# One decode layer on one core: K and V in three rotating 8 MiB tiles of four heads instead of four 4 MiB tiles of two

## The chip, the cores and the metric

One core of a Trainium2 chip runs the whole layer as one program. The metric is the device time of one execution in microseconds (us); the median of three runs counts. A profiled execution comes with it: its own time, and a trace whose times run from the start of the span, that is from the core's first to its last recorded instruction. TensorE is called PE (its weight loads PEld), VectorE DVE, ScalarE ACT, GpSimd POOL, and SyncE, which issues nearly all DMAs, SP.

## The reference

A decode step for batch 2 and one new token: attention over a cache of 8192 keys, with 32 heads of 128, then a gated feed-forward. All inputs are bf16. Cut to what matters:

```python
# x [2,1,512]; k_cache, v_cache [2,32,8192,128]; wq [512,4096]; wo [4096,512]
q = layernorm(x) @ wq                                   # 32 heads of 128
p = softmax(einsum("bhqd,bhkd->bhqk", q, k_cache) * 128 ** -0.5)
h = x + einsum("bhqk,bhkd->bhqd", p, v_cache) @ wo
hn = layernorm(h)                                       # W_gate, W_up [512,1376], W_down [1376,512]
gate = hn @ W_gate
out = h + (gate * (gate > 0) * (hn @ W_up)) @ W_down
```

K and V are 134 MB each and are read once. They are 268 of the 281 MB that the core loads.

## The kernel before

**Steps and tiles.** A step is a pair of heads of one batch entry: 32 steps, `i` = 0 to 31, the last called `L`. The K of a pair is 4 MiB and lies as 128 partitions of 32 KiB (`ROW`): heads side by side in the partitions (64 each), 128 keys (`NT`) of 128 numbers in each partition. `kbuf` and `vbuf` hold two such tiles each, so K of step `i + 2` goes where K of step `i` lay.

**Scores.** Most of the keys of a partition are scored on DVE, in place in the K tile: `products` (L335) multiplies by the query, `scores` (L350) adds halves four times, and a reduction (L354) makes the scores. The rest, 16 of 128 keys (24, 32 and 8 in some steps at the ends), go over PE in `scores_pe`: transposed in chunks of eight (L309), copied by ACT (L311), multiplied by a query laid out with zeros (L300), copied as rows (L316), transposed back (L319) and copied into the column of scores (L325).

**Softmax and values.** A reduction (L358), a matmul (`largest`, L365) and a second reduction (L377) give the largest score; `exponentials` (L380) writes the weights on ACT. `values` multiplies weights and V with 32 matmuls of 512 columns a step, in two parts (L396); ACT copies the result (L402). For each group of four steps `diagonals` (L411) picks the heads out of it, `sums` (L266) adds up the exponentials on PE, `shares` (L270) takes the reciprocal on DVE, and `normalise` (L274) writes the head's columns `ocol`, on DVE too.

**The order of the work is written out by hand**, and every engine takes its instructions in program order. In the loop, step `i` does: `sums(i - 2)`, `scores_pe(i)`, `products(i)`, `shares` and `normalise` of `i - 2` where a group ended there, `values(i - 1, 0)`, `scores(i)`, `largest`, `exponentials`, the load of K for `i + 2`, `values(i - 1, 1)`, `diagonals(i - 1)`, the load of V for `i + 1`. The values are thus one step, and the normalising two steps, behind the scores. All these loads go through SP's queue in order (L133); each first waits until the work that reads or writes the old data of its place is done.

**The weights.** W_q is loaded first, into `wbig`, and W_o after it into the same place while the first K tiles land. W_o is cut into sets (`SETS`): one of 128 KiB lies on 16 partitions only, in four rows of four (L240), the others on 128. `spread` and `attend_set` bring the heads into the matching layout and multiply. After the loop come the last step, with V in four pieces, and the loads of W_gate, W_up and W_down (L522, L526), then the rest of the attention, the second norm and the feed-forward. `values_cols` (L423) does the values of the last two steps with V as the stationary operand.

Of the kernel before, what the change touches and what calls it, by code (L numbers as in the profile page):

```python
# [23 lines left out]
def kernel(  # L24
# [13 lines left out]
    nc = tc.nc  # L38
# [6 lines left out]
    HALF = P // 2  # L45


    NT = 2 * Sk // P
    ROW = NT * Dh
    NG = Hq // 2  # L50
    NPE = NT // 4
    NPE_MID = NT // 8
    NPE_LAST = NT // 16
    TPC = 8
    VG = 4
# [5 lines left out]

    FSETS = [(0, 6), (6 * P, 1), (7 * P, 1), (8 * P, 1), (9 * P, 1), (F - P, 1)]
# [3 lines left out]

    SETS = [(0, 16, P, 0), (16, 1, 16, 16), (17, 1, P, 24), (18, 2, P, 25), (20, 4, P, 27), (24, 4, P, 32)]
    WO_T = 36  # L70
    HM = Hq - 4

    assert Sq == 1 and Hkv == Hq and Dh == P and D == KC * P and Hq == 32 and NPE % TPC == NPE_MID % TPC == NPE_LAST % TPC == 0
    assert F == 11 * P - AGAIN

    big = ctx.enter_context(tc.tile_pool(name="big", bufs=1))
    consts = ctx.enter_context(tc.tile_pool(name="consts", bufs=1))
    small = ctx.enter_context(tc.tile_pool(name="small", bufs=2))
# [3 lines left out]
    big.tile([P, 192], bf16, name="pad")  # L82
    kbuf = big.tile([P, 2, ROW], bf16)
    vbuf = big.tile([P, 2, ROW], bf16)
    wbig = big.tile([P, 40 * D], bf16)
    wd_sb = big.tile([P, FC, D], bf16)
    qrep = consts.tile([P, B, NG, Dh], bf16)

    wq_sb = wbig[:, 0:KC * Hq * Dh].rearrange("p (c n) -> p c n", c=KC)

    wgu = kbuf[:, 0, 0:2 * KC * F].rearrange("p (k c f) -> p k c f", k=2, c=KC)


    pgz = consts.tile([P, 2, NT // VG, 2, VG], bf16)

    pv = consts.tile([P, 2, VG * Dh], f32)
    pick = consts.tile([P, VG, 4, 2], f32)
    zc = consts.tile([P, B, NG, 2], f32)
    ident = consts.tile([P, P], bf16)
    nscale = consts.tile([P, P], f32)  # L100
# [4 lines left out]
    ocol = consts.tile([P, Hq, B], bf16)  # L105
    hm = consts.tile([P, FC, B], bf16)

    SROWS = [n * Dh // w for _, n, w, _ in SETS]
    sizes = [r for r in sorted(set(SROWS)) if r > 1]
    quot = {r: consts.tile([P, Dh // r], bf16, name=f"quot{r}") for r in sizes}  # L110
    rest = {r: consts.tile([P, r], bf16, name=f"rest{r}") for r in sizes}
    orow = [consts.tile([P, r, B], bf16, name=f"orow{k}") for k, r in enumerate(SROWS)]
    placed = consts.tile([P, B, 16], bf16)
    sel = consts.tile([B, B, HALF], bf16)

    QZ = 2 * NPE // 4
    qz = consts.tile([P, B, NG, 2 * QZ], bf16)
    ident_f = consts.tile([QZ, QZ], f32)
# [3 lines left out]

    steps = [(b, g) for b in range(B) for g in range(NG)]
    N = len(steps)

    def wo_set(k):
        return wbig[:, SETS[k][3] * D:]

    def load_kv(cache, buf, i, pieces=1, which=None):
        b, g = steps[i]  # L130
        w = ROW // pieces
        for k in range(pieces) if which is None else which:
            nc.sync.dma_start(  # L133
                out=buf[:, i % 2, k * w:(k + 1) * w],
                in_=_dram(cache, (b * Hkv + 2 * g) * Sk * Dh + k * w, [[ROW, P], [1, w]]),
            )
# [19 lines left out]
    with tc.manual_schedule():  # L156

        xr = wd_sb[0:B, FC - 2, :]
        nc.scalar.dma_start(out=xr, in_=_dram(A_x, 0, [[D, B], [1, D]]))
        nc.sync.dma_start(out=wbig[:, 0:KC * Hq * Dh], in_=_dram(A_wq, 0, [[KC * Hq * Dh, P], [1, KC * Hq * Dh]]))  # L160
        load_kv(A_k_cache, kbuf, 0)
        load_kv(A_k_cache, kbuf, 1)
        load_kv(A_v_cache, vbuf, 0)
# [18 lines left out]
            base=0, pattern=[[-1, B], [0, HALF]], channel_multiplier=1,  # L182
        )
        nc.gpsimd.memset(qz, 0.0)
        nc.gpsimd.memset(pgz, 0.0)
# [4 lines left out]
            base=0, pattern=[[-1, VG], [-32, 4], [-VG, 2]], channel_multiplier=1,  # L190
# [15 lines left out]
        for r in sizes:  # L206
            nc.vector.tensor_reduce(out=rest[r], in_=_free(ident, 0, [[1, r], [r, P // r]]), axis=AXIS.X, op=ALU.max)
            nc.vector.tensor_reduce(out=quot[r], in_=_free(ident, 0, [[r, P // r], [1, r]]), axis=AXIS.X, op=ALU.max)
# [4 lines left out]

        qrow = vbuf[0:B, 1, 0:Hq * Dh]
        for g0 in range(0, NG, 4):
            for n0 in range(2 * g0 * Dh, 2 * (g0 + 4) * Dh, 4 * Dh):
# [6 lines left out]
            for b in range(B):  # L223
                r_ps = ps2.tile([P, 4, Dh], f32, tag="tp")
                for j in range(2):
                    nc.tensor.matmul(  # L226
                        out=r_ps[j * HALF:(j + 1) * HALF], lhsT=sel[:, b, :],
                        rhs=_free(qrow, (2 * g0 + j) * Dh, [[2 * Dh, 4], [1, Dh]]), start=True, stop=True,
                    )
                nc.scalar.activation(out=qrep[:, b, g0:g0 + 4, :], in_=r_ps, func=ACT.Copy)  # L230
# [3 lines left out]
        nc.vector.tensor_copy(qz[:, :, :, QZ - 2:QZ], qT_ps.rearrange("p (g j) b -> p b g j", j=2))  # L234


        for k, ((h0, n, w, _), r) in enumerate(zip(SETS, SROWS)):
            nc.sync.dma_start(
                out=wo_set(k)[0:w, 0:r * D],
                in_=_dram(A_wo, h0 * Dh * D, ([[r * D, P]] if w == P else [[r * D, 4], [4 * r * D, 4]]) + [[1, r * D]]),  # L240
            )
        nc.sync.dma_start(
            out=wbig[:, WO_T * D:(WO_T + Hq - HM) * D].rearrange("p (h n) -> p h n", n=D),
            in_=_dram(A_wo, HM * Dh * D, [[D, P], [Dh * D, Hq - HM], [1, D]]),
        )

        groups = {}
        for b in range(B):
            for g0 in range(0, NG, 4):
                if b == B - 1 and g0 + 4 == NG:  # L250
                    groups[b * NG + NG - 3] = (b, g0, 2)
                    groups[b * NG + NG - 2] = (b, NG - 2, 1)
                    groups[b * NG + NG - 1] = (b, NG - 1, 1)
                else:
                    groups[b * NG + g0 + 3] = (b, g0, 4)
        o_ps = {}
        rzs = {}

        z_ps = {}

        def sums(i):

            if i in groups:
                b, g0, n = groups[i]
                z_ps[i] = ps.tile([P, 2 * n], f32, tag="mx", name="z_ps")
                nc.tensor.matmul(out=z_ps[i], lhsT=ones, rhs=zc[:, b, g0:g0 + n, :], start=True, stop=True)  # L266

        def shares(i):
            rzs[i] = small.tile([P, 2 * groups[i][2]], f32, tag="rz", name="rz")
            nc.vector.reciprocal(out=rzs[i], in_=z_ps[i])  # L270

        def normalise(i):
            b, g0, n = groups[i]
            nc.vector.tensor_tensor(  # L274
                out=ocol[:, 2 * g0:2 * (g0 + n), b], in0=o_ps[i][:, 0:2 * n], in1=rzs[i], op=ALU.mult,
            )

        scols = {}
        L = N - 1

        def share(i):

            npe = NPE_LAST if i == L else NPE if i >= L - 2 else NPE_MID if i else NPE - TPC
            return NT - npe, npe

        def scores_pe(i):


            b, g = steps[i]
            kt = kbuf[:, i % 2, :]  # L290
# [357 lines left out]
```

## Time and profile before

| what | value |
|---|---|
| median of 3 runs | 662.05 us (661.82 to 662.43) |
| profiled execution: its own time, its span | 661.76 us, 660.0 us |
| PE / DVE / ACT / POOL busy | 432.5 / 551.9 / 154.7 / 4.9 us |
| HBM read | 281.09 MB, 426 GB/s over the span |
| K and V loads | 32 of K and 29 of V of 4 MiB, 4 of V of 2 MiB, 4 of V of 1 MiB |
| mean granted TensorE clock | 0.818 of full speed |

Busy times are sums over the whole span, and stages with different limits lie behind them. A PE that is counted busy may be running at half its clock. The 1.76 us between the time and the span lie outside what the trace records.

### The profile page before, as it was taken

The numbers are of one execution on the slowest core, as the hardware profiler recorded it, in microseconds if no ns is written. First come the engines' busy times: TensorE is split into PE (matmuls) and PEld (weight loads), VectorE is DVE, ScalarE is ACT, GpSimd is POOL, SyncE is SP. The second block draws the span as 40 slices with busy tenths as digits, with TensorE's granted clock in tenths as the row PEclk, the third lists the DMA queues.
The fourth block names the chain that finished last, engine by engine and source line by source line (L and its number), as shares of the span: only waits on it lengthen the run. The fifth ranks groups of instructions, "written<-read, shape, count | busy, mean of one in ns | idle before, by whom it ended". The sixth has DMA issues, their size and how long they took to land.

```text
span 660.0 us, 6125 instructions
## 1 busy us (share of the span) xinstructions
PE 432.5 (66%) x2567; PEld 190.8 (29%) x2567; DVE 551.9 (84%) x327; ACT 154.7 (23%) x340; POOL 4.9 (1%) x21
## 2 busy tenths in 40 slices
PE   2725677676666557667656765676676765688676
PEld 1312222322223223222223222232222422234246
DVE  2599998888889888889988888988888998887991
ACT  1421222222122222022222212222221222222410
POOL 2000000000000000000000000000000000000000
PEclk9967987888778898877789877778987778988975
DMA  9999999999999999999999999999999999999996
GB/s 381 434 411 447 427 432 440 420 439 434 429 437 428 437 426 435 439 426 435 436 424 440 427 433 438 427 436 435 425 440 429 430 439 425 439 432 424 430 421 273
DMA packets 13331, 281.48 MB, mean 426 GB/s; under 512 B 1382, under 2 KB 2664, under 8 KB 4200
## 3 DMA queue, kind: packets, MB, share of 16 engines
q1 hardware_dynamic: 13300, 281.09, 99.1%
q8 instruction: 20, 0.33, 0.2%
q14 instruction: 7, 0.06, 0.0%
q10 hardware_dynamic: 4, 0.00, 0.0%
HBM read 281.09 MB, written 0.00 MB: 426 GB/s over the span
## 4 chain that ended last, share of the span: by engine, by line
DMA 52%; DVE 42%; PE 4%; SPq 1%; issue 1%; ACT 0%; DVEq 0%; ACTq 0%
DMA kbuf<-in_A_k_cache_dram 47%; DVE kbuf L350 20%; DVE kbuf L335 19%; DVE scol L354 3%; DMA wd_sb<-in_B_W_down_dram 3%; DMA wbig<-in_A_wq_dram 2%; PE q_ps L219 1%; PE pv_ps L396 1%; SPq L522 1%; DVE vbuf L222 0%; PE r_ps L226 0%; PE mx_ps L365 0%; PE d_ps L606 0%; ACT kT L311 0%; PE row_ps L300 0%
## 5 line engine op out<-in xcount | busy, mean ns | idle before, releaser
L396 PE MATMUL pv_ps<-vbuf,pgz 128*8 128x512 bf16 x960 | 283.5, 462 | 78.0 <-DMA vbuf<-in_A_v_cache_dram 78.0
L335 DVE TENSOR_TENSOR kbuf<-kbuf,qrep 128x14336 bf16<-128x14336 bf16 (+3 forms) x32 | 241.8, 7557 | 40.1 <-DMA kbuf<-in_A_k_cache_dram 40.1
L350 DVE TENSOR_TENSOR kbuf<-kbuf 128x1792 bf16<-128x1792 bf16 (+9 forms) x128 | 242.2, 1892 | 4.1
L396 PEld LDWEIGHTS <-pgz 128*8 128x8 bf16 x960 | 93.3, 100 | 244.1 <-issue 174.5
L380 ACT ACTIVATE pgz<-scol,nm 64x128 bf16<-64x128 f32 x64 | 25.5, 399 | 334.7 <-DVE nm L377 333.9
L311 ACT ACTIVATE kT<-t_ps 128x1024 bf16<-128x1024 bf16 x68 | 66.2, 1021 | 15.1 <-PE t_ps L309 14.6
L300 PE MATMUL row_ps<-kT,qz 128*8 128x512 bf16 (+3 forms) x136 | 42.7, 398 | 33.9 <-ACT kT L311 33.7
L365 PE MATMUL mx_ps<-nscale,pm 128*128 128x128 f32 x64 | 16.5, 343 | 65.4 <-DVE pm L358 63.2
L309 PE MATMUL t_ps<-ident,kbuf 128*128 128x128 bf16 x544 | 37.5, 222 | 0.0
L309 PEld LDWEIGHTS <-kbuf 128*128 128x128 bf16 x544 | 32.1, 100 | 11.8 <-issue 11.7
L354 DVE TENSOR_REDUCE scol<-kbuf 128x112 f32<-128x896 bf16 (+3 forms) x32 | 34.5, 1078 | 1.1
L402 ACT ACTIVATE pv<-pv_ps 8x512 f32<-8x512 f32 x30 | 17.7, 589 | 74.2 <-PE pv_ps L396 74.2
L365 PEld LDWEIGHTS mx_ps<-nscale,pm 128*128 128x128 f32 x64 | 10.5, 206 | 79.9 <-issue 49.0
L377 DVE TENSOR_REDUCE nm<-mx_ps 128x2 f32<-128x128 f32 x32 | 9.3, 291 | 23.8 <-PE mx_ps L365 23.8
L319 PE MATMUL sc_ps<-ident_f,rows 8*128 8x8 f32 (+3 forms) x128 | 14.2, 216 | 21.7 <-ACT rows L316 21.7
L300 PEld LDWEIGHTS <-qz 128*8 128x8 bf16 (+3 forms) x136 | 11.2, 84 | 51.2 <-issue 43.5
L316 ACT ACTIVATE rows<-row_ps 8x512 f32<-8x512 f32 (+3 forms) x32 | 18.8, 587 | 23.4 <-PE row_ps L300 23.4
L319 PEld LDWEIGHTS sc_ps<-ident_f,rows 8*128 8x128 f32 (+3 forms) x128 | 11.3, 149 | 39.5 <-ACT rows L316 39.5
L325 ACT ACTIVATE scol<-sc_ps 64x16 f32<-64x16 f32 (+3 forms) x64 | 12.4, 194 | 17.8 <-PE sc_ps L319 17.0
L222 DVE CAST vbuf<-q_ps 2x512 bf16<-2x512 f32 x8 | 5.4, 678 | 13.2 <-PE q_ps L219 13.2
L219 PE MATMUL q_ps<-wbig,xn 128*2 128x512 bf16 x32 | 9.2, 440 | 8.6 <-DMA wbig<-in_A_wq_dram 8.6
L358 DVE TENSOR_REDUCE pm<-scol 128x1 f32<-128x128 f32 x32 | 9.1, 285 | 3.7 <-DVE scol L354 0.5
(96 smaller groups left out, 112.4 us busy)
## 6 DMA issues: line engine op xcount, KB each, us to landing
kbuf<-in_A_k_cache_dram SPq DMA_DIRECT2D x32, 4096.0 KB, 22.1
vbuf<-in_A_v_cache_dram SPq DMA_DIRECT2D x29, 4096.0 KB, 27.3
vbuf<-in_A_v_cache_dram SPq DMA_DIRECT2D x4, 2048.0 KB, 26.1
wbig<-in_A_wq_dram SPq DMA_DIRECT2D x1, 4096.0 KB, 12.4
vbuf<-in_A_v_cache_dram SPq DMA_DIRECT2D x4, 1024.0 KB, 20.7
wbig<-in_A_wo_dram SPq DMA_DIRECT2D x1, 2048.0 KB, 22.1
wbig<-in_A_wo_dram SPq DMA_DIRECT2D x3, 512.0 KB, 22.1
kbuf<-in_B_W_gate_dram SPq DMA_DIRECT2D x1, 1376.0 KB
```

Of the source, the lines that this page charges most:

```text
L300: nc.tensor.matmul(out=row_ps, lhsT=qz[:, b, g, z0:z0 + 2 * U], rhs=kTs[c0][:, k * P:(k + 4) * P], start=(u == 0), stop=(u == U - 1),)
L309: nc.tensor.transpose(t_ps[:, k, :], kt[:, t * Dh:(t + 1) * Dh], ident)
L311: nc.scalar.activation(out=kTs[c0], in_=t_ps.rearrange("p t s -> p (t s)"), func=ACT.Copy)
L316: nc.scalar.activation(out=rows, in_=row_ps, func=ACT.Copy)
L319: nc.tensor.transpose(sc_ps[:, t].rearrange("p u j -> p (u j)"), rows[:, t * P:(t + 1) * P], ident_f[0:2 * U, 0:2 * U],)
L335: nc.vector.tensor_tensor(out=kv, in0=kv, in1=_free(qrep, (b * NG + g) * Dh, [[0, nv], [1, Dh]]), op=ALU.mult,)
L350: nc.vector.tensor_tensor(out=lo, in0=lo, in1=_free(kt, half, [[Dh, nv], [1, half]]), op=ALU.add,)
L354: nc.vector.tensor_reduce(out=scol[:, 0:nv], in_=_free(kt, 0, [[Dh, nv], [1, 8]]), axis=AXIS.X, op=ALU.add,)
L365: nc.tensor.matmul(out=mx_ps.rearrange("p a b -> p (a b)"), lhsT=_free(pms[i], 0, [[0, P]]), rhs=nscale, start=True, stop=True,)
L380: nc.scalar.activation(out=pgz[r, s, :, j, :], in_=scol[r, :].rearrange("p (u t) -> p u t", t=VG), func=ACT.Exp, scale=SCALE, bias=nm[r, j ...
L396: nc.tensor.matmul(out=pv_ps[i][r, :], lhsT=pgz[:, s, u].rearrange("p j t -> p (j t)"), rhs=vbuf[:, s, u * VG * Dh:(u + 1) * VG * Dh], sta ...
L402: nc.scalar.activation(out=pv[r, (g // 4) % 2], in_=pv_ps[i][r, :], func=ACT.Copy)
```

## The change

A step becomes four heads: a K or V tile is 8 MiB, 64 KiB in each partition (256 keys; a head has 32 partitions). Three tiles `bufs[0..2]` rotate: K0, V0, K1, V1 and so on take them in turn, so V of step `i + 1` goes where K of step `i` lay, and K of step `i + 2` where V of step `i` lay. There are 15 steps of four heads (0 to 14, the last called `Q`); the last four heads are two more steps of a pair, `p0` and `p1`. DVE scores 240 of the 256 keys, PE 16 (48 of 256, 32 of 128 and 16 of 128 in the last three steps).

The PE part of the scores keeps its transposed keys and its rows in the K tile itself. One query layout `qz` is filled for each step by a small copy on POOL (`place_q`). Values now follow the scores in the same step. A group's `sums`, `shares` and `normalise` come in the next step, behind `scores_pe` and `products`. W_q, W_o and the feed-forward weights have no place of their own any more and use parts of the three tiles. W_o is loaded near the end, as three sets and four heads, all on 128 partitions. The bodies of `products`, `scores`, `largest`, `exponentials`, `values`, `diagonals` and `values_cols` do the same work as before on the new shapes.

The diff, cut to its core (new lines of the loop and the tail in full, the old ones left out there):

```diff
-    NT = 2 * Sk // P
-    ROW = NT * Dh
-    NG = Hq // 2
-    NPE = NT // 4
-    NPE_MID = NT // 8
-    NPE_LAST = NT // 16
-    TPC = 8
-    VG = 4
     EPS = 1e-5
...
+    NH = 4
+    NQ = Hq // NH
+    LASTQ = B * NQ - 2
+    TILE = NH * Sk * Dh // P
+    HALF = TILE // 2
+    TPC = 8
+    VG = 4
+    NPE = 16
+    NPE_END = {LASTQ: 48, LASTQ + 1: 32, LASTQ + 2: 16}
+    QZ = 48
+    SETS = [(0, 16, 0), (16, 8, 16), (24, 4, 24)]
+    HM = 28
+    SROWS = [n for _, n, _ in SETS]
...
-    kbuf = big.tile([P, 2, ROW], bf16)
-    vbuf = big.tile([P, 2, ROW], bf16)
-    wbig = big.tile([P, 40 * D], bf16)
-    wd_sb = big.tile([P, FC, D], bf16)
-    qrep = consts.tile([P, B, NG, Dh], bf16)
...
+    bufs = [big.tile([P, TILE], bf16, name=f"tile{k}") for k in range(3)]
...
+    wq_sb = bufs[2][:, 0:HALF].rearrange("p (c n) -> p c n", c=KC)
+    qrow = bufs[2][0:B, HALF:HALF + Hq * Dh]
+    xr = bufs[2][0:B, HALF + Hq * Dh:HALF + Hq * Dh + D]
+    wo = bufs[1][:, HALF:TILE]
+    wgu = bufs[2][:, HALF:HALF + 2 * KC * F].rearrange("p (k c f) -> p k c f", k=2, c=KC)
+    wd_sb = bufs[0][:, 0:FC * D].rearrange("p (c n) -> p c n", c=FC)
...
+    class Step:
+        def __init__(self, i):
+            self.i = i
+            self.quad = i <= LASTQ
+            if self.quad:
+                self.b, self.g = divmod(i, NQ)
+                self.nh, self.nt = NH, TILE // Dh
+                self.kt, self.vt = bufs[2 * i % 3], bufs[(2 * i + 1) % 3]
+                self.qr = qrep[:, i, :]
+                self.pg, self.zc = pgq, zc[:, self.b, self.g, :]
+            else:
+                k = i - LASTQ - 1
+                self.b, self.g, self.k = B - 1, NQ - 1, k
+                self.nh, self.nt = 2, HALF // Dh
+                self.kt = bufs[0][:, k * HALF:(k + 1) * HALF]
+                self.vt = bufs[1 + k][:, 0:HALF]
+                self.qr = qpair[:, k, :]
+                self.pg, self.zc = pgp[:, k], zc[:, self.b, self.g, 2 * k:2 * k + 2]
+            self.npe = NPE_END.get(i, NPE)
+            self.nv = self.nt - self.npe
+            self.hp = P // self.nh
...
-        load_kv(A_k_cache, kbuf, 0)
-        load_kv(A_k_cache, kbuf, 1)
-        load_kv(A_v_cache, vbuf, 0)
+        nc.sync.dma_start(out=bufs[2][:, 0:HALF], in_=_dram(A_wq, 0, [[KC * Hq * Dh, P], [1, KC * Hq * Dh]]))
+        load_tile(A_k_cache, steps[0], steps[0].kt)
+        load_tile(A_v_cache, steps[0], steps[0].vt)
...
+        load_tile(A_k_cache, steps[1], steps[1].kt)
...
-        for k, ((h0, n, w, _), r) in enumerate(zip(SETS, SROWS)):
-            nc.sync.dma_start(
-                out=wo_set(k)[0:w, 0:r * D],
-                in_=_dram(A_wo, h0 * Dh * D, ([[r * D, P]] if w == P else [[r * D, 4], [4 * r * D, 4]]) + [[1, r * D]]),
-            )
-        nc.sync.dma_start(
-            out=wbig[:, WO_T * D:(WO_T + Hq - HM) * D].rearrange("p (h n) -> p h n", n=D),
-            in_=_dram(A_wo, HM * Dh * D, [[D, P], [Dh * D, Hq - HM], [1, D]]),
-        )
...
+        def place_q(s):
+            nc.gpsimd.tensor_copy(qz[:, QZ - NH:QZ], qTs[:, s.b, NH * s.g:NH * (s.g + 1)])
+        groups = {3: (0, 0, 4), 7: (0, 4, 4), 11: (1, 0, 4), 13: (1, 4, 2), 14: (1, 6, 1)}
...
-                kTs[c0] = small.tile([P, TPC * P], bf16, tag="kT", name="kT", bufs=2)
-                nc.scalar.activation(out=kTs[c0], in_=t_ps.rearrange("p t s -> p (t s)"), func=ACT.Copy)
+                    nc.tensor.transpose(t_ps[:, k, :], s.kt[:, t * Dh:(t + 1) * Dh], ident)
+                nc.scalar.activation(
+                    out=s.kt[:, (nv + c0) * Dh:(nv + c0 + TPC) * Dh], in_=t_ps.rearrange("p t s -> p (t s)"), func=ACT.Copy,
...
+            rows = s.kt[0:nh * U, nv * Dh:nv * Dh + 8 * P].bitcast(f32)
...
+        place_q(steps[0])
+        for i in range(Q):
+            s = steps[i]
+            scores_pe(s)
+            place_q(steps[i + 1])
+            products(s)
+            if i - 1 in groups:
+                sums(i - 1)
+                shares(i - 1)
+                normalise(i - 1)
+            if i == 12:
+                lay_rows(0, spread(0))
+            scores(s)
+            load_tile(A_v_cache, steps[i + 1], steps[i + 1].vt)
+            largest(s)
+            exponentials(s)
+            values(s, 0)
+            values(s, 1)
+            if i in groups:
+                diagonals(i)
+            if i + 2 <= Q:
+                load_tile(A_k_cache, steps[i + 2], steps[i + 2].kt)
+            else:
+                for t in steps[Q + 1:]:
+                    load_tile(A_k_cache, t, t.kt)
+        s, p0, p1 = steps[Q:]
+        scores_pe(s)
+        products(s)
+        sums(Q - 1)
+        shares(Q - 1)
+        normalise(Q - 1)
+        lay_rows(1, spread(1))
+        scores(s)
+        load_tile(A_v_cache, p0, p0.vt)
+        for k, (h0, n, at) in enumerate(SETS):
+            nc.sync.dma_start(
+                out=wo[:, at * D:(at + n) * D], in_=_dram(A_wo, h0 * Dh * D, [[n * D, P], [1, n * D]]),
+            )
+        nc.sync.dma_start(
+            out=wo[:, HM * D:Hq * D].rearrange("p (h n) -> p h n", n=D),
+            in_=_dram(A_wo, HM * Dh * D, [[D, P], [Dh * D, Hq - HM], [1, D]]),
+        )
+        largest(s)
+        exponentials(s)
+        scores_pe(p0)
+        products(p0)
+        values(s, 0)
+        scores_pe(p1)
+        scores(p0)
+        largest(p0)
+        exponentials(p0)
+        values(s, 1)
+        load_tile(A_v_cache, p1, p1.vt, pieces=4)
+        for w, src, n in ((0, B_W_gate, 1), (1, B_W_up, KC // 2)):
             for c in range(0, KC, n):
                 nc.sync.dma_start(
                     out=wgu[:, w, c:c + n], in_=_dram(src, c * P * F, [[F, P], [P * F, n], [1, F]]),
                 )
+        for f0, n in FSETS[-1:] + FSETS[:-1]:
+            fc = FC - 1 if f0 == F - P else f0 // P
+            nc.sync.dma_start(out=wd_sb[:, fc:fc + n, :], in_=_dram(B_W_down, f0 * D, [[n * D, P], [1, n * D]]))
+        diagonals(Q)
+        products(p1)
+        sums(Q)
+        shares(Q)
+        normalise(Q)
+        values_cols(p0, 0, p0.nt)
+        attend_set(0)
+        attend_set(1)
+        scores(p1)
+        largest(p1)
+        exponentials(p1)
+        late = spread(2)
+        sums(Q + 1)
+        shares(Q + 1)
+        normalise(Q + 1)
+        lay_rows(2, late)
+        attend_set(2)
+        values_cols(p1, 0, p1.nt // 2)
         for h in range(HM, HM + 2):
             attend(h)
+        sums(Q + 2)
+        shares(Q + 2)
+        values_cols(p1, p1.nt // 2, p1.nt)
+        normalise(Q + 2)
         for h in range(HM + 2, Hq):
             attend(h)
```

## The prediction

> **What bounds the kernel now.** The page first: the slices of the DMA row, the granted clock, the chain.
>
> ```profile
> PEclk9967987888778898877789877778987778988975
> DMA  9999999999999999999999999999999999999996
> ...
> DMA 52%; DVE 42%; PE 4%; SPq 1%; issue 1%; ACT 0%; DVEq 0%; ACTq 0%
> ```
>
> The DMA engines are full until the last slice. The chain hops between K's landings and DVE, so I ask who waits for whom (DVE's and SP's waits; us in total, times, longest):
>
> ```profile
> DVE kbuf L335 <- DMA kbuf<-in_A_k_cache_dram: 40.1, 28, 2.2
> ...
> SPq L133 <- DVE scol L354: 424.9, 30, 17.8
> SPq L133 <- PE pv_ps L396: 137.7, 33, 6.8
> ```
>
> DVE waits for K, 1.4 us a step. SP waits for buffers, but that costs nothing as long as queued loads keep the engines full: in the chain a K load issued at 195.89 lands 22.1 later, though 4 MiB take only half of that. K loads are issued every 38.7 us per two steps (195.89, 234.62): four tiles of 4 MiB, 433.7 GB/s. With the odd longer pair the mean is 38.9, from (584.62 - 117.87) / 12. So this kernel is bound by the stream with some 12 us of loads queued when K's place comes free. The question is whether the change keeps that reserve.
>
> **What the new loads save.** The trace's DMA records give 1213 ns for a 32 KiB packet, 611 for 16 KiB, 309 for 8 KiB: 9 ns are fixed. Halving 8192 packets over 16 engines saves at most 256 x 9 ns = 2.3 us, and nothing if a row is still cut in two; I take 1. W_o's set in four rows of four is a load that four engines could carry: 32 KiB each, 1.2 us instead of 0.3. Near the end the DMA share is 0.76 (652 to 654), then 0.54, so some engines finish late: spreading it is worth 0.9 us, while the stream sets the end.
>
> **A step of four heads.** DVE's rows by form (mean ns after the comma):
>
> ```profile
> L335 DVE TENSOR_TENSOR kbuf<-kbuf,qrep 128x14336 bf16<-128x14336 bf16 x28 | 213.5, 7625 | 38.2 <-DMA kbuf<-in_A_k_cache_dram 38.2
> L350 DVE TENSOR_TENSOR kbuf<-kbuf 128x7168 bf16<-128x7168 bf16 x28 | 108.9, 3889 | 0.8
> L354 DVE TENSOR_REDUCE scol<-kbuf 128x112 f32<-128x896 bf16 x28 | 30.4, 1086 | 1.0
> ...
> L335 DVE TENSOR_TENSOR kbuf<-kbuf,qrep 128x15360 bf16<-128x15360 bf16 x1 | 8.1, 8149 | 0.0
> ```
>
> An element costs 0.52 ns in L335, 0.525 in L350 and 1.05 in L354. For 240 keys: product 16.1 (30720 elements), sums 8.2 + 4.2 + 2.2 + 1.2, reduction 2.2; with gaps 34.1 us from start to K's release, and 1.7 more for the maximum. DVE needs 35.8 of 38.9: it stays under the stream. But V of the next step goes into this K's place, and K of the next step, already loading, ends 38.7 after this one. So 4.6 us are queued at the release instead of 12. A restart costs 1.1: W_q's issue began at 0.73, its first packet at 1.8.
>
> From K's release to the first exponential 1.4 us pass now (reduction over at 195.83, exponential at 197.25); I add 0.4 for 256 columns and a cold `largest`. Four exponentials at about 0.62 (0.52 apart now, 0.1 for 128 more columns): the values start 4.4 after the release, 38.5 after K's landing. They are 64 matmuls in one go, on a PE that has rested since `scores_pe`. The windows view (PE busy and count first, the clock behind POOL):
>
> ```profile
> 131.00:136.40 5.40, 5.40 (x13) 1.61 (x13) 5.30 (x4) 0.00 (x0) 0.00 (x0) 0.50 1.02 443
> 138.90:142.50 3.60, 3.60 (x19) 1.36 (x19) 2.16 (x2) 0.98 (x4) 0.00 (x0) 1.00 1.01 437
> ```
>
> After a rest a matmul takes 0.427 us (weight loads so far apart) at half clock; warm, 16 take 3.6, or 0.22 each. The cold stretch lasted 4.1, 4.6, 5.5 and 3.4 us where values began after a wait (91.64, 111.67, 130.99, 150.31). With 4: 9 cold, 55 warm, 16.0 us (15.3 to 16.8). V's place is free at 34.1 + 4.4 + 16.0 + 1.1 = 55.6, and needed at 58.05, after three tiles of 19.35: an ordinary step loses nothing, if values stay under 18.4.
>
> The Trainium skill (TensorE: Matmul & The Clock Gate, Part 1: The HAM clock gate) calls the ramp under 1% of a typical span and not worth modelling; 215.7 ns a matmul would make the values 13.8, and my sum about 683 (each group 3.2 less, the tail 6.4). The cold windows here decide for 16.
>
> **Where a group ended: steps 4, 8, 12 and `Q`.** This is the dear part. DVE's `shares(i - 1)` now stands behind `products(i)`, and its `sums` on PE behind the values of step i - 1, `diagonals` and all of `scores_pe(i)`. The trace has that row of work, with `sums` before the transposes:
>
> ```profile
> 196.75 3.62 PE L396 MATMUL pv_ps<-vbuf,pgz 128*8 128x512 bf16 x16
> ...
> 201.05 1.06 PE L411 MATMUL o_ps<-pick,pv 128*128 128x8 f32 x8 [0.68 <-ACT pv L402]
> 201.96 0.37 PE L266 MATMUL z_ps<-zc,ones 128*128 128x8 f32 x2
> 202.18 1.05 PE L309 MATMUL t_ps<-ident,kbuf 128*128 128x128 bf16 x16
> ...
> 206.09 0.41 PE L319 MATMUL sc_ps<-ident_f,rows 8*128 8x8 f32 x4 [0.68 <-ACT rows L316]
> 206.20 0.20 DVE L270 RECIPROCAL rz<-z_ps 128x8 f32<-128x8 f32 x1
> ```
>
> Values end at 200.37, the last transposes at 206.50: 6.1 us, 6.8 in an earlier group. I take 6.8 with `sums`. DVE finds its sum ready here and doesn't wait. After the change the values end 54.5 after K's landing, 15.8 into the next step; `sums` is done at 22.6; DVE ends its product at 16.2 and stands 6.4 us, with the four additions behind it. K comes free at 22.6 + 0.4 + 17.95 = 40.95, V's load starts at 42.05 where the stream ran dry at 38.7: 3.35 us of gap. Values end at 61.35, the next K starts at 62.45 instead of 58.05. So 4.4 us are lost, with 0.5 for slow first packets 4.9 (the first 16 packets of the run took 1.75 us on average against 1.21). Nothing gives it back. Three times 14.7, and 0.6 for `spread(0)` at step 12: 15.3.
>
> K0 lands at 32.5 (13.1 for W_q, and 19.35), after the queries are ready (28.7 now, with about the same instructions). Step 14 starts at 32.5 + 14 x 38.9 + 15.3 = 592.4.
>
> **The tail, from there.** The values of 13 end at 14.9. `diagonals` 1.75, `scores_pe` with six chunks 9.3 (four took 6.8 from 610.10, two 4.3), `sums` 0.4: 26.3. DVE's product of 208 keys ended at 14.1, so it stands 12 us. With `shares`, `spread(1)` 1.0 and 15.7 of additions K is free at 43.0; V of p0, W_o and V of p1 stream from 44.1 to 73.2, the feed-forward weights to 83. But the engines are later. PE: exponentials until 47.4, `scores_pe(p0)` behind them on ACT until 53.3, half the values 9.0, `scores_pe(p1)` 4.3, `largest(p0)` at 67.1. DVE has been ready with p0 since 59; it does p1's product until 75.1, waits for `sums(Q)`, behind the second half of the values (76.1), until 78.3, and ends p1's scores at 88.0. From that point to `hc` (L556) it took 7.9 now (640.90 to 648.79), and 11.2 more to the end, 1.2 of it waits for weights that here have long landed: 88.0 + 7.9 + 10.0 = 105.9. W_o's balance is worth nothing there.
>
> Sum: 592.4 + 105.9 = 698.3, and 1.8 outside the span (661.76 against 660.0), less 1 for packets: **699 us**. The profiled execution before took 661.76, 0.3 under the median, so the sum needs no other shift.
>
> POOL's `place_q` comes after `scores_pe(i)` and is needed by `scores_pe(i + 1)`, over 30 us later; should it hold DVE up, that is 0.1 to 0.3 a step (POOL's small memsets and selects), inside DVE's 3 us of slack. The PE part's copies into the K tile replace equal ones: nothing. W_o's four loads only change their place in SP's queue, ahead of p1's V: 9.7 us of the same stream.
>
> **Rivals.**
> - *The stream still sets everything* (not slower). If DVE's wait at a group is under 3.5 us (4.6 queued less 1.1), no load starts late, and the tail is hidden: 577.1 + 77.6 of stream + 1 + 4.5 after the last landing, 1.8 outside, less 2 for packets and W_o: 660. For it: DMA is full in every slice now. Against it: `sums` would have to be done by 19.7, and 64 warm matmuls alone end at 13.6, with 6.8 behind them. 6%.
> - *The groups cost, the tail hides* behind the loads: 592.4 + 83 + 1 + 4.5 + 1.8 = 682. It needs DVE's tail 20 us shorter. 10%.
> - *Ordinary steps lose too*: cold PE for longer. Two steps' K are tied by 59.0 + values; at 20 us that is 79.0 against 77.4, 0.8 a step, and about 5 more at each group: near 725. The trace's cold stretches end after 5.5 us. 9%.
> - *Rows twice as far apart load slower*: at 3% the steps take 40.1, less a shorter stall at groups: 712. Packets of 8, 16 and 32 KiB show one rate, so 3%. The Trainium skill (DMA: Bandwidth & Descriptors, Latency and other measured facts) has copies slow down at row pitches of powers of two, 207 GB/s at 512 KiB and 103 at 4 MiB; no run here has such a pitch.
>
> **Numbers.** My forecast gets 72%: 686 (values of 15.3, a warm tail) to 712 (16.8, restarts twice as dear). The range 680 to 716 adds the second and fourth rival. Faster by over 0.2% (about what a measurement of this kernel can tell from no change, 1.3 us) 5%, within it 2%, slower 93%.
>
> **What would show it.** Right: DMA below 9 in slices near 200, 360 and 520 us; DVE idle before `shares` by `sums` about 6 us three times and 12 once; K landings 38.9 apart, 43.8 after a group's step; DMA idle for the last 20 us. Wrong: no idle DVE in front of the reciprocals in `shares`, or gaps at every step.

## The result and the profile after

The changed kernel takes **698.28 us** (median of 5 runs, 697.46 to 698.5) against 662.05 (661.82 to 662.43 in the 5 runs beside it): 1.0545 of the time before, 95% interval 1.053 to 1.0561. The forecast was 699.0. The profiled execution took 698.5 us, with a span of 696.6.

The same three rows of the page as before, the granted clock, the DMA share in 40 slices and the chain that ended last:

```profile
PEclk9755866859596685958677595957768595885985
DMA  9999999999999799999999799999999799996990
...
DVE 47%; PE 27%; DMA 19%; ACT 5%; issue 1%; DVEq 0%; ACTq 0%
```

The DMA row now has four holes before the end: the slices at 226 to 244, 383 to 400, 540 to 557 and 627 to 644 us, one behind each of the steps 4, 8, 12 and `Q`, and the last 17 us are empty. The chain that was 52% DMA is 19% DMA; DVE (47%) and PE (27%) carry most of it. The waits of DVE and of SP's queue (us in total, times, longest):

```profile
DVE tile L351 <- DMA tile<-in_A_k_cache_dram: 48.8, 12, 6.6
DVE rz L293 <- PE z_ps L289: 31.2, 7, 10.9
...
SPq L157 <- DVE scol L364: 318.4, 15, 40.7
SPq L157 <- PE pv_ps L399: 293.7, 19, 20.6
```

The second line is new in the loop: the reciprocal of `shares` waits for the sums on PE. In the kernel before it waited only at the very end, 0.28 and 3.27 us:

```profile
DVE rz L270 <- PE z_ps L266: 3.5, 2, 3.3
```

Its seven waits are now 6.10 (step 4), 3.81 (8), 5.73 (12), 10.86 (`Q`), 1.14, 0.28 and 3.27 us. DVE itself costs what was expected (groups by form):

```profile
L351 DVE TENSOR_TENSOR tile<-tile,qrep 128x30720 bf16<-128x30720 bf16 x14 | 226.2, 16156 | 43.9 <-DMA tile<-in_A_k_cache_dram 43.9
L362 DVE TENSOR_TENSOR tile<-tile 128x15360 bf16<-128x15360 bf16 x14 | 114.2, 8156 | 0.4
L364 DVE TENSOR_REDUCE scol<-tile 128x240 f32<-128x1920 bf16 x14 | 30.1, 2153 | 1.4
```

Step 4 in the timeline (start, duration, engine, line; in brackets the idle time before and what ended it):

```profile
190.31 16.20 PE L399 MATMUL pv_ps<-tile,pgq 128*16 128x512 bf16 x64 [2.94 <-ACT pgq L385]
190.58 16.16 DVE L351 TENSOR_TENSOR tile<-tile,qrep 128x30720 bf16<-128x30720 bf16 x1 [2.88 <-DMA tile<-in_A_k_cache_dram]
...
207.19 1.06 PE L411 MATMUL o_ps<-pick,pv 128*128 128x16 f32 x8 [0.68 <-ACT pv L404]
208.10 1.05 PE L324 MATMUL t_ps<-ident,tile 128*128 128x128 bf16 x16
...
212.41 0.40 PE L289 MATMUL z_ps<-zc,ones 128*128 128x16 f32 x2
...
212.84 0.26 DVE L293 RECIPROCAL rz<-z_ps 128x16 f32<-128x16 f32 x1 [6.10 <-PE z_ps L289]
...
231.35 0.33 SPq L157 DMA_DIRECT2D tile<-in_A_v_cache_dram  x1
```

DVE's product ends at 206.74, and the values of step 3 on PE at 206.51. The diagonals, two chunks of transposes and the sums follow, and DVE stands until 212.84. So K comes free late and V's load is issued at 231.35. By the DMA records the 16 engines had run out between 227.95 and 230.37, and begin again from 232.31 on. The windows view (the last three columns are the clock, the DMA share and GB/s; a packet counts where it starts) shows the hole, and the clock ramp inside the values:

```profile
189.50:199.00 9.50, 8.69 (x30) 3.15 (x31) 8.42 (x1) 0.73 (x4) 0.00 (x0) 0.72 0.90 386
201.00:206.60 5.60, 5.51 (x26) 2.11 (x24) 5.60 (x1) 0.05 (x1) 0.00 (x0) 1.00 1.03 445
228.00:232.00 4.00, 0.22 (x1) 0.22 (x2) 3.52 (x3) 0.00 (x0) 0.00 (x0) 0.50 0.00 0
```

### The profile page after: what moved, and what is told of

Read it like the earlier page. It is cut to its first block, busy times and chain, and to the rows that moved or that the text cites. A ratio compares the mean times of both kernels' runs of the same rounds, so it can differ in the third digit from the quotient of the medians.

```text
span 696.6 us, 5060 instructions
## 1 busy us (share of the span) xinstructions
PE 344.7 (49%) x2137; PEld 160.7 (23%) x2137; DVE 560.4 (80%) x193; ACT 114.1 (16%) x277; POOL 67.6 (10%) x40
## 4 chain that ended last, share of the span: by engine, by line
DVE 47%; PE 27%; DMA 19%; ACT 5%; issue 1%; DVEq 0%; ACTq 0%
DVE tile L362 26%; PE pv_ps L399 18%; DMA tile<-in_A_k_cache_dram 17%; DVE tile L351 16%; DVE scol L364 3%; ACT pgq L385 3%; DMA tile<-in_A_wq_dram 2%; ACT tile L325 2%; PE mx_ps L375 1%; PE q_ps L240 1%; PE row_ps L315 1%; PE t_ps L324 1%; PE o_ps L411 1%; DVE pm L368 1%; DVE nm L380 1%
## 5 line engine op out<-in xcount | busy, mean ns | idle before, releaser
L351 DVE TENSOR_TENSOR tile<-tile,qrep 128x30720 bf16<-128x30720 bf16 (+1 forms) x15 | 240.2, 16014 | 48.8 <-DMA tile<-in_A_k_cache_dram 48.8
L399 PE MATMUL pv_ps<-tile,pgq 128*16 128x512 bf16 x960 | 239.2, 416 | 41.1 <-ACT pgq L385 41.1
L362 DVE TENSOR_TENSOR tile<-tile 128x15360 bf16<-128x15360 bf16 (+7 forms) x68 | 246.7, 3627 | 2.2
L399 PEld LDWEIGHTS <-pgq 128*16 128x16 bf16 x960 | 91.2, 96 | 185.4 <-ACT pgq L385 45.2
L271 POOL COPY qz<-qTs 128x4 bf16<-128x4 bf16 x15 | 62.5, 4170 | 489.3 <-PE row_ps L315 489.3
L385 ACT ACTIVATE pgq<-scol,nm 32x256 bf16<-32x256 f32 x60 | 30.3, 505 | 254.0 <-DVE nm L380 252.8
L325 ACT ACTIVATE tile<-t_ps 128x1024 bf16<-128x1024 bf16 x40 | 39.1, 1021 | 24.4 <-PE t_ps L324 24.0
L364 DVE TENSOR_REDUCE scol<-tile 128x240 f32<-128x1920 bf16 (+2 forms) x16 | 33.0, 2061 | 1.6
L315 PE MATMUL row_ps<-tile,qz 128*16 128x512 bf16 (+1 forms) x68 | 20.9, 391 | 14.7 <-ACT tile L325 14.6
L324 PE MATMUL t_ps<-ident,tile 128*128 128x128 bf16 x320 | 24.0, 232 | 6.8 <-DMA tile<-in_A_k_cache_dram 6.8
L351 DVE TENSOR_TENSOR tile<-tile,qpair 128x12288 bf16<-128x12288 bf16 (+1 forms) x2 | 14.2, 7082 | 0.0
```

The source lines that it names most:

```text
L271: nc.gpsimd.tensor_copy(qz[:, QZ - NH:QZ], qTs[:, s.b, NH * s.g:NH * (s.g + 1)])
L315: nc.tensor.matmul(out=row_ps, lhsT=z, rhs=s.kt[:, (nv + c0 + k) * Dh:(nv + c0 + k + 4) * Dh], start=(u == 0), stop=(u == U - 1),)
L324: nc.tensor.transpose(t_ps[:, k, :], s.kt[:, t * Dh:(t + 1) * Dh], ident)
L325: nc.scalar.activation(out=s.kt[:, (nv + c0) * Dh:(nv + c0 + TPC) * Dh], in_=t_ps.rearrange("p t s -> p (t s)"), func=ACT.Copy,)
L351: nc.vector.tensor_tensor(out=kv, in0=kv, in1=_free(s.qr, 0, [[0, s.nv], [1, Dh]]), op=ALU.mult)
L362: nc.vector.tensor_tensor(out=lo, in0=lo, in1=_free(s.kt, half, [[Dh, s.nv], [1, half]]), op=ALU.add)
```

## The experiments

Times are medians; each ratio is against runs of the kernel before on the same chip. Unless said otherwise a diff, shortened here, is against the changed kernel. In the expectations e3 is experiment 3, e4 is 9, e6 is 5, e11 is 10 and e14 is 11. A PE is called cold where the granted clock is 0.5 and warm where it is 1.0; a DMA engine has run dry when it has no queued packet left.

**1. The groups of the loop behind the exponentials.**

```
-            if i - 1 in groups: sums, shares, normalise(i - 1)
-            if i == 12: lay_rows(0, spread(0))
             scores(s)
             ...
             exponentials(s)
+            if i - 1 in groups: sums, shares, normalise(i - 1)
+            if i == 12: lay_rows(0, spread(0))
             values(s, 0)
```

> The changed kernel with the group's sums, shares and normalise (and step 12's spread) of the loop moved behind exponentials of the same step, where the sum has long been possible; the tail is untouched. If DVE's wait for sums makes the loop's loss, the three waits of 6.1 us and the dry stream after them go: step 14 starts some 15 us earlier, 683 us (679 to 687). If the loss lies in thin reserves at every step or in the tail alone, 695 to 698.

688.65 us, ratio 1.0397 (1.0381 to 1.0414): 9.6 less, between the two forecasts. The waits at 4, 8 and 12 are down to 0.7 us, and step 14 starts at 584.75 instead of 595.53. That is less than the 15 of the sum, and the steps show why: all 14 together are now 39.4 us apart on average (38.6 to 40.4), not 38.6 to 38.9.

**2. The same for the last group, in `Q`'s block.**

```
-        sums(Q - 1) ... lay_rows(1, spread(1))     (ahead of scores(s))
         exponentials(s)
+        sums(Q - 1) ... lay_rows(1, spread(1))
         scores_pe(p0)
```

> The changed kernel with the same block moved behind exponentials only in step Q (group 13, with its spread and lay_rows). If the tail is a chain of DVE and PE, K of step 14 is free 11.8 us earlier and the block costs 1.7 later: 688 us. If the late load of p0's V makes the tail (5 us of dry stream), 693. If the tail hides it, 698.

689.74 us, ratio 1.0415 (1.0395 to 1.0436): 8.5 less, nearest to the 688 of a tail that is a chain of DVE and PE. Step 14 now lasts 32.9 us to p0's product instead of 43.0.

**3. Both.**

> Both moves. If the two losses are separate they add: 673 us (669 to 677). If one hides behind the other, 680 or more.

677.07 us, ratio 1.0225 (1.0199 to 1.0251). The two together are worth 21.2 us, against 18.2 for the sum of the two alone; the runs of this version lie 4.1 us apart, so the difference may be noise. The two losses add, but the time is 4 us over the 673 expected, and 15 us over the kernel before are left, with no long wait for sums in the loop to explain them (0.7 each; the longest is 3.3, at the very end). The trace's DMA records say more: between 40 and 600 us an engine is empty for 3.0 us (12.7 in the changed kernel, 0.0 before), but 288 packets of 64 KiB took over 2.48 us instead of 2.42 (half of them 2.74 or more, nine in ten under 3.3), which is 7.5 us per engine (as in the changed kernel; 0.6 before, in packets of 32 KiB). They stand at the seams between loads: 7.2 of the 7.5 us are packets that start within 6 us after the issue of a K or V load, half of it behind each kind. Theory: engines run out there, because the reserve is thin.

**4. W_o's balance alone**, in the kernel before:

```
-    SETS = [(0, 16, P, 0), (16, 1, 16, 16), (17, 1, P, 24), (18, 2, P, 25), (20, 4, P, 27), (24, 4, P, 32)]
-    WO_T = 36
+    SETS = [(0, 16, P, 0), (16, 8, P, 16), (24, 4, P, 24)]
+    WO_T = 28
```

> The kernel before with one part of the change alone: W_o as three sets and four heads, all on 128 partitions. If the set in four rows of four delays the last engines, 0.9 us less: 661.1. If the spread of the engines' ends has other causes (instruction loads), 662.0.

662.44 us (11 runs), ratio 1.0004 (0.9995 to 1.0013): no gain; 0.9 us less lies outside the interval.

**5. A larger reserve**, on top of experiment 3: `NPE = 32` instead of 16, that is 32 keys of each partition scored on PE.

> e3_both_late with 32 instead of 16 keys of each head's share on PE in the steps 0 to 13. DVE's scores of a step become shorter by 16 x 128 elements of L351, the sums and the reduction, 2.25 us; K comes free 2.25 sooner, so that 6.9 us instead of 4.6 are queued then. e3 has no 6 us waits in the loop any more, yet its steps are 39.4 us apart on average and its DMA engines spend 7.5 us each on packets slower than 2.42 us. Theory (the thin reserve: some engines run out before V's load starts and begin again with packets of 3.0 to 3.3 us): steps of 38.8, so 13 x 0.55 = 7 us less, 670 (668 to 673), and the slow packets fall to a third. Rival (39.4 is what 8 MiB in rows of 64 KiB take; reserve plays no part): 677 within 1.5, slow packets as before. Rival (PE's 2.5 us more per step delays the values): slower than 677.

668.58 us, ratio 1.0099 (1.0084 to 1.0114): 8.5 less than experiment 3, the time of the first theory. Nearly all steps are 38.6 us apart. From V's issue to the landing of the next K, which is what is queued at K's release, it is now 6.4 to 6.8 us in all steps but one, where it was 4.2 to 7.0. The waits of DVE for K grow (51.7 us in experiment 3), since DVE is done earlier. The DMA row has no holes before its last slice (compare those above), but neither has that of experiment 3: what is new shows in the packets.

```profile
DVE tile L351 <- DMA tile<-in_A_k_cache_dram: 73.6, 15, 6.7
```
```profile
DMA  9999999999999999999999999999999999999992
```

The slow packets fall from 288 to 51 and their cost from 7.5 to 0.9 us per engine. The four runs lie within 0.7 us of each other, those of experiment 3 within 4.1. The values are no shorter (15.7 to 16.9 us in the loop, 15.3 to 16.9 in experiment 3), so a warmer PE is not the cause. The rest of the loop's loss was the thin reserve. Which reserve, this run doesn't tell: DVE done sooner brings forward both K's release and the values, so V's release too.

**6. Longer values**, on top of experiment 3:

```
             values(s, 0)
+            extra(24, lambda u: s.vt[:, u * VG * Dh:(u + 1) * VG * Dh])
             values(s, 1)
```

> e3_both_late with 24 more matmuls behind the 64 of values in the steps 0 to 13; they read the same V and write to a PSUM tile that nobody reads, so the result is the same and V's place comes free some 5.3 us later (16 becomes 21.3). The prediction has a threshold at values of 18.4 us. Theory: beyond it V's landing of two steps is tied by 59.0 + values; 59.0 + 21.3 - 77.4 = 2.9 per two steps, 1.45 a step, against 77.4, +20 us; against e3's own 78.7 per two steps it is 0.8 a step, +11. So 688 to 697. Rival (the stream of the loads sets the ordinary steps and the values are hidden): 677 within 2.

695.59 us, ratio 1.0517 (1.049 to 1.0544): 18.5 more, inside the range of the theory, but by luck. The values of steps 0 to 13 last 20.0 us on average (18.8 to 22.1) instead of 16.0: 4.0 longer and not 5.3, for which the rule of the expectation gives some 2 us over experiment 3 (59.0 + 20.0 against 78.7 per two steps), or 11 over steps of 38.7. All of them lie past the prediction's threshold of 18.4, and from the second on every step is 39.8 us or more; where exactly the threshold lies, no run shows. What the rule has too small is the way from the values' end to the next K in that place, 20.45 us (1.1 and 19.35): it took 21.7 to 25.4. The DMA row has holes all along the loop.

```profile
DMA  9999979998999979999899998999899997999992
```

**7. A warm PE**, in the changed kernel: `extra(16, ...)` on half-added K during the last additions, `extra(12, ...)` on the identity behind `largest(s)`.

> The changed kernel with PE kept busy before the values: 16 matmuls that read the half-added K (columns 16 to 31 of each key) during the last additions, and 12 that read the identity behind largest; they write to a PSUM tile that nobody reads. The result is the same. My sum for the group stalls uses values of 16.0 with 9 cold matmuls; warm they would be 64 x 0.22 = 14.1. Theory: values of 14.0 to 14.4 instead of 15.6 to 16.8; the sums of steps 4, 8, 12 come 2 us sooner, DVE's 6.1 us waits become 4, three times 2 = 6 us less; V's place comes free 2 us sooner in every step, which gives some of the ordinary steps' loss back: 3 more. 698.3 becomes 689 (686 to 693). Rival (the clock plays no part: matmuls are paced by their weight loads): values stay at 15.6 to 16.8 and the time at 698 within 1.5, or above it by the extra matmuls.

687.63 us, ratio 1.0394 (1.0378 to 1.0409): 10.7 less, as the theory had it, by matmuls whose results nobody reads. The values of step 3 and DVE's wait in step 4, in its timeline:

```profile
189.16 13.98 PE L406 MATMUL pv_ps<-tile,pgq 128*16 128x512 bf16 x64 [0.25 <-ACT pgq L392]
```
```profile
209.74 0.26 DVE L293 RECIPROCAL rz<-z_ps 128x16 f32<-128x16 f32 x1 [3.12 <-PE z_ps L289]
```

13.98 instead of 16.20, and 3.12 instead of 6.10; the other waits fall by 1.8, 2.0 and 2.8 us. The mean granted clock of the run is 0.803 instead of 0.726. In its trace the three pairs of steps that hold a group take 241.0 us instead of 247.3, and the tail 98.9 instead of 101.1. The 3 us expected of the ordinary steps did not come: they stay 39.3 apart. This run brings forward V's release alone, and tells the two reserves apart: the slow packets behind the issue of K's loads, which go where V lay, fall from 3.6 to 0.4 us per engine, those behind V's loads grow from 3.4 to 4.0. So K's reserve alone, left thin, is enough to hold the ordinary steps at 39.3; V's alone was not tested.

**8. More keys on PE and nothing else**: `NPE = 32` in the changed kernel.

> The changed kernel, its order untouched, with 32 instead of 16 keys on PE in the steps 0 to 13. By the prediction's sum: K comes free 2.25 us sooner (31.85 after its landing), the values end at 52.25, but scores_pe of four chunks instead of two takes 2.5 more, so that the sums of a group are done at 22.7 into the step as before, while DVE's product ends at 15.1: the wait at steps 4, 8, 12 grows from 6.1 to 7.5. Behind it 16.75 instead of 17.95 of additions: V's load starts at 40.9 instead of 42.05, the gap shrinks by 1.2 and the next K's landing is 1.2 less late: 3.5 us less for three groups. In the ordinary steps the reserve is 6.9 instead of 4.6: 11 x 0.5 = 5.5 less. 698.3 becomes 689 (686 to 692). Rival (what a group costs goes by DVE's wait alone): 4 us more for the groups, 696 to 699.

694.24 us, ratio 1.0484 (1.0467 to 1.0502): 4 less, not 9, between the two theories. By its trace the gain comes from the tail alone, where DVE's wait in `Q` is 5.61 instead of 10.86; step 14 starts at 596.67, 1.1 later than in the changed kernel. In the loop the wait was foreseen, the price was not:

```profile
210.64 0.26 DVE L293 RECIPROCAL rz<-z_ps 128x16 f32<-128x16 f32 x1 [7.46 <-PE z_ps L289]
```

Away from the groups the steps are 38.6 apart, as expected. But the two steps of each group are 7.9, 6.1 and 8.5 us over 77.2, 22.5 in all (15.7 in the changed kernel: 6.6, 3.1 and 6.0). One of them, by the issues on SP's queue and the DMA records: the engines ran out between 224.8 and 226.4, V's load was issued at 228.02; the K load behind it was issued at 248.97, just as they ran out again, and DVE could start at 273.21, 24.2 us later, where 8 MiB take 19.35:

```profile
273.21 15.09 DVE L351 TENSOR_TENSOR tile<-tile,qrep 128x28672 bf16<-128x28672 bf16 x1 [10.04 <-DMA tile<-in_A_k_cache_dram]
```

Fifteen engines began their first K packets around 250 and were done near 270; one began at 252.3, took 3.68 us for that packet, and was done at 272.9 (the records don't name the engines; they are told apart by packets that follow on each other's end). A load is as late as its last engine, and here two loads in a row began dry.

**9. to 12. The tail**, where experiment 5 left 6.5 us. Experiment 9 is in the order of experiment 3, 10 to 12 with `NPE = 32` as well:

```
 9   exponentials(p0) ahead of scores_pe(p1); sums, shares, normalise(Q) behind exponentials(p1)
10   as 9; also largest(p1), exponentials(p1) ahead of values_cols(p0), attend_set(0), attend_set(1)
11   as 10, but values_cols(p0) ahead of scores(p1)
12   as 11; the block of step Q - 1 moved behind products(p1)
```

> With both moves of e3_both_late in place, the tail's order is changed as well: largest(p0) and its exponentials stand ahead of scores_pe(p1) on PE and ACT, and the sums, shares and normalisation of Q go behind exponentials(p1). In e3 DVE stood 6.5 us for largest(p0) (633.5 to 640.07) and 2.2 us for the sums of Q inside p1's scores; p1's scores were done at 659.7, and the end came 17.5 later. Theory (in the tail DVE sets the end): p1's product starts at 635.9 instead of 640.3, p1's scores end 6.6 us sooner, 677.1 becomes 670.5 (668 to 673). Rival (the last weights set the end: W_down's issue at 652 and its landings up to 662 stay where they are): 675 to 677.

None of these four came out at one of its forecasts. 678.35 us, ratio 1.0245 (1.0223 to 1.0267): no gain. p1's product began 16.7 us after p0's instead of 21.5, but its exponentials then waited 7.56 us for `largest(p1)`, which stood on PE behind 9.25 us of cold values, `values_cols(p0)` and the two `attend_set`.

> e6_more_keys_on_pe with the tail in another order: largest(p0) and exponentials(p0) ahead of scores_pe(p1), as in e4_tail_order, and largest(p1) and exponentials(p1) ahead of values_cols(p0) and the two attend_set. In e4 DVE gained 8 us for p1 but then stood 7.6 us for largest(p1), queued on PE behind values(s, 1) (9.25 us, cold), values_cols(p0) and attend_set. Theory (PE's row of work sets the tail now): exponentials(p1) some 5 us sooner, but 6.7 us of PE work come after them instead of before, so values_cols(p1) starts 2 us sooner than in e6: 668.6 becomes 666.5 (664.5 to 668). Rival (the exponentials of p1 set the end): 663 to 664. In neither case is it faster than the kernel before: its stream alone ends at 660.

670.21 us, ratio 1.0123 (1.0108 to 1.0138): 1.6 worse than experiment 5. The values ran warm this time (7.07), PE rested 3.4 us before `largest(p1)`, and `values_cols(p0)` and the two `attend_set` then stood ahead of `values_cols(p1)`, which began at 652.46 (651.38 in experiment 5).

> e11_keys_and_tail with values_cols(p0) ahead of scores(p1) again, the two attend_set still behind exponentials(p1). In e11 PE stood 3.4 us (638.8 to 642.1) for p1's largest and had values_cols(p0), 3.5 to 4.4 us, behind it: values_cols(p1) began at 652.5. Theory (PE's row of work behind exponentials(p1) sets the end): values_cols(p0) falls into that rest, values_cols(p1) begins at 648.5 to 649, and 670.2 becomes 666.5 (665 to 668). Rival (the last loads set the end): not faster than e11; but there the DMA share falls below 0.1 at 654, 13 us before the end.

668.73 us, ratio 1.0104 (1.0088 to 1.0119). `values_cols(p1)` began at 650.20, later than foreseen, and its second half stopped before its last matmul:

```profile
652.57 1.82 PE L422 MATMUL o_ps<-pgp,tile 128*128 128x2 bf16 x63
656.36 0.18 PE L422 MATMUL o_ps<-pgp,tile 128*128 128x2 bf16 x1 [1.98 <-issue]
```

`largest(p1)` had such a stop of 1.27 us between its two matmuls, from 643.2 on. In the DMA records a 16 KiB packet of the instruction queue starts at 642.1, and another at 654.1 and takes 0.96 us: the stops come beside loads of code. That they cause them wasn't tested. Experiment 5 has such stops too, of 1.21 and 1.02 us, with such packets at 641.1 and 654.3. The two of this run are 3.3 us together; its time missed the forecast by 2.2.

> e14_tail_again with the block of step Q - 1 (sums, shares, normalise, spread(1), lay_rows(1)) taken out from between exponentials(Q) and p0's product: its sums go behind scores_pe(p1) on PE, the rest behind p1's product on DVE, lay_rows(1) behind values(Q, 1). Theory: p0's product begins 1.5 us sooner (0.7 of waiting and 0.9 of work), p1's scores end 0.6 sooner, e14 less 0.5 to 1.5. Rival (p0 and p1 are not what the end waits for): e14 within 0.5. The lower bound for both is the stream: its DMA share falls at 654, and 4.5 us stood behind that in the kernel before, 660 in all.

670.31 us, ratio 1.0126 (1.0109 to 1.0143): 1.6 worse, with ranges that just overlap. p0's product began 1.4 us sooner than in experiment 11 (608.34 against 609.74), p1's 0.5 later (626.15 against 625.64): `largest(p0)` stands behind PE's values, and DVE's wait for it grew from 0.93 to 2.47. The moved work then lay inside p1's scores. No version beat the kernel before.

## Why the prediction was right, and where its terms were off

**What bounds the kernel.** Right, and shown by experiments 3, 5 and 6: with 6.4 us queued at K's release (6.9 in the sum) the stream sets the loop, with 4.2 to 4.5 in steps whose K comes on time (4.6 in the sum) it no longer does, and with values longer by 4.0 us nearly every step pays. (The two issues that the prediction names give 433.2 GB/s, not 433.7; nothing hangs on it.) The account of the 36.2 us by experiments 3 and 5:

| | us |
|---|---|
| waits for sums in the four steps (698.28 to 677.07) | 21.2 |
| the thin reserve in all steps (677.07 to 668.58) | 8.5 |
| the tail behind the last loads (668.58 to 662.05) | 6.5 |

That the rest is the tail, the DMA records show: in experiment 5 the last packets of the weights land at 654.5 us, 2.0 before those of the kernel before (656.5), yet the span ends 7.1 later (667.1 against 660.0).

**A step of four heads.** DVE's terms hold: 16.16, 8.16 and 2.15 measured against 16.1, 8.2 and 2.2. The values were put at 16.0; those of steps 0 to 13 took 16.1 on average (15.3 to 16.8). What did not hold is "an ordinary step loses nothing, if values stay under 18.4". Outside the group pairs the changed kernel's eight steps are 39.3 apart instead of 38.9: 3.4 us. A reserve that is enough by the sum was not enough in the run, and experiment 5 shows that a larger one is; that it fails because single engines run out before the others is read from the packets, not tested.

**The groups.** DVE's wait was put at 6.4 and was 6.10, 3.81 and 5.73. The three pairs of steps took 247.3 us, which is 13.9 over six steps of 38.9, against 15.3 in the sum. Step 14 began at 595.53 instead of 592.4: 1.1 because K0 came later (33.6 for 32.5), 3.4 for the ordinary steps, less 1.4 for the groups. One by one the pairs lost 6.0, 2.5 and 5.4, where each was put at 4.9 (the last at 5.5, with `spread(0)`). With the waits as they were the sum would have 4.6, 2.3 and 4.8: the pairs cost more than their waits give, and the short wait at step 8 hid it in the total, which is luck. The term that is too small is the 0.5 for slow packets. Behind the three holes the first 16 packets took 3.13, 3.08 and 3.14 us instead of 2.42, which is 0.7, and the slow packets behind the K load that follows add 0.3 to 0.5. Experiment 8 shows it more plainly.

**The clock.** The Trainium skill (TensorE: Matmul & The Clock Gate, Part 1: The HAM clock gate) has the ramp at under 1% of a typical kernel's span, and the sum with warm values was 683, an estimate. Experiment 7 is the test: a warm PE is worth 10.7 us, 1.5% of the time, in a kernel whose PE is busy for half of the span. Here the ramp comes back in every step, and at the groups its 2 us stand on the way to a load's issue.

**The tail.** 105.9 in the sum, 101.1 measured (595.53 to 696.6). The mis-sized term is "half the values 9.0": both halves, from 648.66 and from 660.40 on, ran at a granted clock of 1.00 and took 7.07 each, right behind a `scores_pe`. That is 3.9 of the 4.8. `sums(Q - 1)` was done at 24.9 instead of 26.3, and DVE's wait there was 10.86 instead of 12, but this was lost again: `scores_pe(p0)` ended at 53.2, against 53.3 in the sum. These 4.8 us and the 3.1 of the loop partly cancel, and it is luck that the total lies closer than its parts.

**Packets and W_o.** A row of 64 KiB is one packet of 2418 ns, against two of 1213: 8 ns saved per pair, as taken. So the rival of rows twice as far apart falls. The Trainium skill (DMA: Bandwidth & Descriptors, Latency and other measured facts) has copies slow down at some pitches; at 64 KiB no run shows it. The 0.9 us for W_o's balance in the kernel before were wrong: experiment 4 gives 0.3 more, within its interval. What makes some engines finish late there stays open.

**The rivals.** *The stream still sets everything* needs a wait under 3.5; it was 3.8 to 6.1. *The tail hides* needed 20 us less. *Ordinary steps lose too* is in part true: 0.4 a step, half its price, but for another reason, since the values were no longer than forecast.

## What to carry to other kernels

Larger tiles in fewer buffers saved 8 ns in 2426 here and cut what is queued when a place comes free from 12 us to under 5: work out that reserve, in us of stream, before the sizes. With a thin reserve, look for every wait between a load's landing and the release of its place, and put a group's closing work behind the release; here that order alone was worth 21 us. The same holds for each kind of place: here K's and V's were both thin. A cold matmul engine on that way costs too, and matmuls whose results nobody reads can be cheaper than its ramp.

## What the runs showed of the hardware

DMA engines that have run dry are slow with their next 64 KiB packet: after the hole at step 4 of the changed kernel the 16 first packets took 3.13 us on average instead of 2.42. In experiment 8 one engine stayed behind the others after that, and a load that was issued just as they ran out landed 23.9 us after its issue, where its stream alone takes 19.35.

POOL's copy of 128x4 elements can last as long as the DVE instruction beside it:

```profile
37.75 12.05 POOL L271 COPY qz<-qTs 128x4 bf16<-128x4 bf16 x1 [10.30 <-PE row_ps L315]
...
211.46 0.19 POOL L271 COPY qz<-qTs 128x4 bf16<-128x4 bf16 x1 [35.31 <-PE row_ps L315]
```
```profile
33.59 16.16 DVE L351 TENSOR_TENSOR tile<-tile,qrep 128x30720 bf16<-128x30720 bf16 x1 [6.63 <-DMA tile<-in_A_k_cache_dram]
```

The first of these copies ended at 49.80, DVE's instruction at 49.75. So it is with all 11 of the 15 copies that began while a TENSOR_TENSOR (L351 or L362) ran on DVE: they ended 0.04 to 0.05 us behind it, after 2.6 to 12.05 us. The four that found DVE idle took 0.19. The prediction had thought of the other direction, POOL holding up DVE. The held copies cost no time, since they are needed some 30 us later.
